# Where the K transposes of the next head stand in VectorE's program order

## The chip, the core and the metric

The kernel runs on one core of one Trainium2 chip. The metric is the device time in microseconds (us). Before the change, the first three runs took 420.04, 422.7 and 420.0 us (median 420.04).

## The reference, cut to what matters

Two layers work on a batch of four single tokens. Each layer is a grouped-query attention step over a long K and V cache, then a gated feed-forward block. Both layers read the same caches and weights.

```python
# B=4, Hq=32, Hkv=8, Sk=4096, Dh=128, D=512, F=1792, all bfloat16
def attention(x, k_cache, v_cache, wq, wo):
    q = heads(x @ wq)
    scores = einsum(q, repeat(k_cache)) * Dh ** -0.5
    o = einsum(softmax(scores), repeat(v_cache))
    return o @ wo
x = x + attention(layernorm(x), K, V, wq, wo)
x = x + glu(layernorm(x), w_gate, w_up, w_down)
x = x + attention(layernorm(x), K, V, wq, wo)
x = x + glu(layernorm(x), w_gate, w_up, w_down)
```

## The kernel before

One step of the main loop handles one KV head (called head n, 0 to 7 in layer 0 and 8 to 15 in layer 1). It needs four K tiles and four V tiles of 1 MiB, one for each batch row. The tiles live in a ring of 11 slots. A load is issued when a slot comes free, in the fixed order K(n), V(n), K(n+1), V(n+1), and so on. K slots come free after `scores(n)`, V slots after `values(n)`. Layer 1 walks the heads backwards, so that its first head (8) uses the tiles of head 7 again. These eight slots are therefore kept across the layers.

A small scheduler puts operations on engine queues in the order in which the Python code names them, and adds the semaphore waits that the data needs.

```python
ring = [sb(f"ring{i}", [P, T * DH], bf) for i in range(NS)]        # NS = 11

def done_with(n, kind):
    for b in range(B):
        if n == G - 1:                                   # head 7: kept for head 8
            slots[n + 1, kind, b] = slots[n, kind, b]
        else:
            free.append(slots[n, kind, b])
    pump()                                               # issues the next loads

def q_proj(n):
    ...                                                  # PE: Q_ps <- wq, xT
    S.put("act", ... qT[qi] <- Q_ps)
    ...                                                  # PE: Q_ps <- perm, qT
    S.put("act", ... qbd <- Q_ps)

def transpose_k(n, b):                                   # in place, as 32-bit words
    v = ring[slots[n, "k", b]][:].bitcast(dt.int32)
    S.put("dve", lambda e: e.transpose(v, v), ...)

def softmax(n):
    S.put("dve", ... ml <- max(S_ps))
    S.put("dve", ... nbias <- ml)
    S.put("act", ... p_sb <- exp(S_ps))

def weights(n):                                          # merges the four parts of a row
    S.put("dve", ... tr <- ml); S.put("dve", ... nM); S.put("dve", ... dd)
    S.put("act", ... ee <- exp(dd))
    S.put("dve", ... el, den, rden, wt, wcol)

# ... scores, probs_t, values, merge, merge_sum and y_proj are cut ...

def keys_of(n):
    if n != G:
        for b in range(B):
            transpose_k(n, b)
    scores(n); done_with(n, "k"); softmax(n); probs_t(n); weights(n)

def values_of(n):
    values(n); done_with(n, "v"); merge(n); merge_sum(n); y_proj(n)

for l in range(NLAYER):
    for n in range(l * G, (l + 1) * G - 2):
        keys_of(n)
        q_proj(n + 1)
        values_of(n)
    n = (l + 1) * G - 2
    keys_of(n); q_proj(n + 1); keys_of(n + 1); values_of(n); values_of(n + 1)
    # ... residual, feed-forward, next layer's norm and first q_proj ...
```

Of the kernel before, what the change touches and what calls it, by code (L numbers as in the profile page):

```python
# [91 lines left out]
def bass_interleave_layers__gqa_block_cached__glu_gated_glu__decode_kernel(nc, A_x, A_k, A_v, A_wq, A_wo, B_x, B_wg, B_wu, B_wd, out):  # L92
    B, SQ, D = A_x.shape
    _, G, SK, DH = A_k.shape
# [7 lines left out]
    NLAYER = 2  # L102
# [156 lines left out]
    def done_with(n, kind):  # L259


        for b in range(B):
            if n == G - 1:
# [3 lines that stand above are left out]
        pump()  # L267
# [102 lines left out]
    def layer_norm_q():  # L370
        layer_norm(mean_b, "mean_b", float(DH), rs_q, "rs_q")
# [4 lines left out]
    def q_proj(n):  # L376
        g = groups[n][1]
        qi = n % 2
        fns = []
        for h in range(R):  # L380
            for k in range(KD):
                c0 = (g * R + h) * DH
                fns.append(lambda e, h=h, k=k, c0=c0: e.matmul(  # L383
                    Q_ps[:, h * B:(h + 1) * B], lhsT=wq[:, k, c0:c0 + DH], rhs=xT[:, k, :],
                    start=(k == 0), stop=(k == KD - 1),
                ))
        S.put("pe", fns, reads=["xT", f"wq{g // 2}"], writes=["Q"])
        S.put("act", lambda e: e.activation(qT[qi][:], Q_ps[:, 0:R * B], ACTF.Copy), reads=["Q"], writes=[f"qT{qi}"])  # L388
        fns = []
        for n in range(NQ):  # L390
            fns.append(lambda e, n=n: e.matmul(  # L391
                Q_ps[:, 64 + n * 16:64 + (n + 1) * 16], lhsT=perm[:, n, :], rhs=qT[qi][:], start=True, stop=True,
            ))
        S.put("pe", fns, reads=[f"qT{qi}", "perm"], writes=["Q"])
        fns = []
        for a in range(4):
            fns.append(lambda e, a=a: e.activation(  # L397
                qbd[32 * a:32 * a + 32, qi, :, :, a * R:(a + 1) * R],
                Q_ps[32 * a:32 * a + 32, 64:128].rearrange("p (n h b) -> p b n h", n=NQ, h=R),
                ACTF.Copy,  # L400
            ))
        S.put("act", fns, reads=["Q"], writes=[f"qbd{qi}"])

    def transpose_k(n, b):
        s = slots[n, "k", b]
        v = ring[s][:].bitcast(dt.int32)
        S.put("dve", lambda e: e.transpose(v, v), reads=[f"r{s}"], writes=[f"r{s}"])  # L407

    def scores(n):
        qi = n % 2  # L410
        fns = []
        for q in range(2):
            for nn in range(NQ):
                for b in range(B):
                    kt = ring[slots[n, "k", b]][:].rearrange("p (t bb j r) -> p t bb j r", bb=2, j=32, r=2)
                    fns.append(lambda e, q=q, nn=nn, b=b, kt=kt: e.matmul(  # L416
                        S_ps[32 * b:32 * b + 16, q * 512:(q + 1) * 512],
                        lhsT=qbd[:, qi, b, nn, :],
                        rhs=kt[:, 16 * q:16 * q + 16, nn // 2, :, nn % 2],
                        start=(nn == 0), stop=(nn == NQ - 1),  # L420
                    ))
        S.put("pe", fns, reads=[f"qbd{qi}"] + [f"r{slots[n, 'k', b]}" for b in range(B)], writes=["S"])

    def softmax(n):
        S.put(
            "dve", lambda e: e.tensor_reduce(ml[:, 0:1], S_ps[:], AX.X, ALU.max, negate=True),  # L426
            reads=["S"], writes=["ml"],
        )
        S.put("dve", lambda e: e.tensor_scalar(nbias[:], ml[:, 0:1], rs_q[:], None, op0=ALU.mult),  # L429
              reads=["ml", "rs_q"], writes=["nbias"])  # L430
        S.put(
            "act",
            lambda e: e.activation(  # L433
                p_sb[:].rearrange("p tb (j q) -> p q tb j", q=4),
                S_ps[:].rearrange("p (q tb j) -> p q tb j", q=4, tb=8),
                ACTF.Exp, bias=nbias[:], scale=rs_q[:], accum_out=ml[:, 32:33],
            ),
            reads=["S", "nbias"], writes=["p_sb", "ml_l"],
        )

    def probs_t(n):
        pt = pt_sb[n % 2]
        fns = []
        for tb in range(8):
            fns.append(lambda e, tb=tb: e.matmul(  # L445
                PT_ps[:, tb * 64:(tb + 1) * 64], lhsT=p_sb[:, tb, :], rhs=sel_p[:], start=True, stop=True,
            ))
        S.put("pe", fns, reads=["p_sb", "sel_p"], writes=["PT"])
        S.put(
            "act", lambda e: e.activation(pt[:].rearrange("p t x -> p (t x)"), PT_ps[:], ACTF.Copy),  # L450
            reads=["PT"], writes=[f"pt_sb{n % 2}"],
        )

    def weights(n):
        S.put("dve", lambda e: e.transpose(tr[:], ml[:]), reads=["ml", "ml_l"], writes=["tr"])  # L455
        nm = tr[:, 0:16].rearrange("p (a h) -> p a h", h=R)
        ls = tr[:, 32:48].rearrange("p (a h) -> p a h", h=R)

        def bc(t):
            return t[:].unsqueeze(1).broadcast_to([P, 4, R])  # L460

        S.put(
            "dve",
            lambda e: e.tensor_reduce(nM[:], tr[:, 0:16].rearrange("p (a h) -> p h a", h=R), AX.X, ALU.min),
            reads=["tr"], writes=["nM"],
        )
        S.put("dve", lambda e: e.tensor_tensor(dd[:], bc(nM), nm, ALU.subtract), reads=["nM", "tr"], writes=["dd"])
        S.put("act", lambda e: e.activation(ee[:], dd[:], ACTF.Exp, scale=rs_q[:]), reads=["dd", "rs_q"],  # L468
              writes=["ee"])
        S.put("dve", lambda e: e.tensor_tensor(el[:], ee[:], ls, ALU.mult), reads=["ee", "tr"], writes=["el"])  # L470
        S.put(
            "dve", lambda e: e.tensor_reduce(den[:], el[:].rearrange("p a h -> p h a"), AX.X, ALU.add),
            reads=["el"], writes=["den"],
        )
        S.put("dve", lambda e: e.reciprocal(rden[:], den[:]), reads=["den"], writes=["rden"])
        S.put(
            "dve",
            lambda e: e.tensor_tensor(
                wt[:, 0:16].rearrange("p (a h) -> p a h", h=R), ee[:], bc(rden), ALU.mult
            ),  # L480
            reads=["ee", "rden"], writes=["wt"],
        )
        wc = wcol[n % 2]
        S.put("dve", lambda e: e.transpose(wc[:], wt[:]), reads=["wt"], writes=[f"wcol{n % 2}"])
# [27 lines left out]
    def merge_sum(n):  # L512

        _, g = groups[n]
        src = bass.AP(M_ps, 0, [[512, P], [32, B], [1, R], [P + R, 4]])
        dst = oT[:, g * R:(g + 1) * R, :].rearrange("p h b -> p b h")

        def fn(e):
            with nc.allow_low_precision("the heads' outputs enter the projection as bfloat16"):
                return e.tensor_reduce(dst, src, AX.X, ALU.add)  # L520

        S.put("dve", fn, reads=["M"], writes=[f"oT{g}"])

    def y_proj(n):
        _, g = groups[n]
        i = n % G
        fns = []
        for h in range(R):
            for j in range(4):
                fns.append(lambda e, h=h, j=j: e.matmul(  # L530
                    Y_ps[32 * j:32 * j + B, 0:P], lhsT=oT[:, g * R + h, :], rhs=wo[:, g * R + h, j * P:(j + 1) * P],
                    start=(i == 0 and h == 0), stop=(i == G - 1 and h == R - 1),
                ))
        S.put("pe", fns, reads=[f"oT{g}", f"wo{g // 2}"], writes=["Y"])
# [63 lines left out]
        residual(rs_h[:], ["rs_h"], last)  # L598


    def keys_of(n):

        if n != G:
            for b in range(B):
                transpose_k(n, b)
        scores(n)
        done_with(n, "k")
        softmax(n)
        probs_t(n)
        weights(n)  # L610

    def values_of(n):
        values(n)
        done_with(n, "v")
        merge(n)
        merge_sum(n)
        y_proj(n)

    layer_norm_q()
    q_proj(0)  # L620
    for l in range(NLAYER):
        for n in range(l * G, (l + 1) * G - 2):
            keys_of(n)
            q_proj(n + 1)
            values_of(n)
        n = (l + 1) * G - 2
        keys_of(n)
        q_proj(n + 1)
        keys_of(n + 1)
        values_of(n)  # L630
        values_of(n + 1)
        residual(1.0, [])
        glu(l == NLAYER - 1)
        if l < NLAYER - 1:
            layer_norm_q()
            q_proj(n + 2)
# [51 lines left out]
```

## Time and profile before

| | before |
|---|---|
| time, median of three | 420.04 us |
| layer 0, 10 to 210 us | 396 GB/s, DMA share 1.04 |
| layer 1, 240 to 340 us | 349 GB/s, DMA share 0.91 |
| start to start of the scores in layer 1 | 23.9 to 24.35 us |

These are three lines of the page of the kernel before: the busy line of the engines, then the DMA share (in tenths) and the GB/s in 40 slices of the span.

```profile
PE 165.4 (39%) x1998; PEld 69.7 (17%) x1998; DVE 192.5 (46%) x272; ACT 85.2 (20%) x171; POOL 9.4 (2%) x34
...
DMA  8999999999999999999940797979989797989220
GB/s 318 399 378 416 388 392 401 398 407 380 415 386 399 397 404 422 411 339 395 400 206 2 284 406 262 398 292 382 383 296 408 284 403 303 401 314 355 63 87 2
```

No engine is half busy. The loads run flat out in the first half. After a pause between the layers (slices 21 and 22) they swing between 262 and 408 GB/s, until they end.

The next lines are the stretches view of the kernel before. After the borders of a stretch and its length come the busy us (and instructions) of PE, PEld, DVE, ACT and POOL, the granted PE clock, the DMA share and GB/s.

```profile
10.00:210.00 200.00, 74.06 (x862) 30.24 (x866) 96.86 (x121) 39.78 (x81) 0.86 (x2) 0.63 1.04 396
240.00:340.00 100.00, 41.71 (x476) 16.89 (x472) 48.33 (x62) 20.80 (x41) 0.00 (x0) 0.58 0.91 349
```

Layer 0 is bound by loading, and layer 1 is not. In layer 0 it is a near tie: the scores of its heads 3 to 5 start 23.8 and 23.9 us apart (96.22, 120.06, 143.97), about the pace of layer 1, while the loads leave no gap. What holds layer 1 is read from the chain of waits of the kernel before, here for one head. The columns are start, length, and the work.

```profile
267.69 8.81 DVE ring L407 x4
...
276.54 3.62 PE S_ps L416 x31
...
280.18 1.24 DVE ml L426
...
281.74 2.63 ACT p_sb L433 x2
...
284.41 0.62 PE PT_ps L445 x8
...
286.25 3.56 PE O_ps L492 x31
...
289.91 0.70 ACT o_sb L504
...
290.65 1.13 PE M_ps L509 x4
...
291.81 0.23 DVE oT L520
292.03 2.21 DVE ring L407
```

This is a closed loop of compute with no load in it: transposes, scores, softmax, values, merge, and the next head's transposes. The four transposes are 8.8 of its 24.3 us. The waits view of the kernel before says the same. The columns are the total, the number of waits and the longest, in us.

```profile
PE S_ps L416 <- DVE ring L407: 132.5, 15, 11.2
...
PE Q_ps L391 <- ACT qT L388: 8.3, 16, 0.6
...
DVE ring L407 <- DMA ring<-in_A_k_cache_dram: 4.0, 9, 1.8
```

PE waits 132.5 us for transposes, and the transposes wait only 4.0 us for their data. This view is of the whole span: 73.1 of the 132.5 us lie between 10 and 210 us, in layer 0.

### The profile page before, as it was taken

Reading aid. Unit: us, or ns where it says so; the run is one execution under the profiler, and the core shown is the slowest. Engines: PE = TensorE matmul, PEld = TensorE weight load, DVE = VectorE, ACT = ScalarE, POOL = GpSimd, SP = SyncE. Lnnn points to the kernel's source line nnn. Section 1 sums busy time; section 2 is a strip of 40 time slices with the busy share of each in tenths; the row PEclk is TensorE's granted clock in tenths of the full one; section 3 lists DMA queues with packets and bytes.
Section 4 is the critical chain, followed back from the end, with each engine's and each line's share of the span. In section 5 each row is a group of like instructions: output and inputs, shape, how many; then the busy total and the mean of one; then the engine's idle time right before and its main releaser. Section 6 shows DMA issues by size and latency. Waiting matters only on the chain.

```text
span 418.9 us, 4800 instructions
## 1 busy us (share of the span) xinstructions
PE 165.4 (39%) x1998; PEld 69.7 (17%) x1998; DVE 192.5 (46%) x272; ACT 85.2 (20%) x171; POOL 9.4 (2%) x34
## 2 busy tenths in 40 slices
PE   0153350524435251405376514536251533531364
PEld 0121020201202020102134201103020210201022
DVE  3825418263452727392011272552728254466512
ACT  1040130402204040303011403103040302204031
POOL 6000000000000000000000000000000000000000
PEclk9985565666666566556565555565566666656579
DMA  8999999999999999999940797979989797989220
GB/s 318 399 378 416 388 392 401 398 407 380 415 386 399 397 404 422 411 339 395 400 206 2 284 406 262 398 292 382 383 296 408 284 403 303 401 314 355 63 87 2
DMA packets 48549, 140.04 MB, mean 334 GB/s; under 512 B 2192, under 2 KB 6544, under 8 KB 40848
## 3 DMA queue, kind: packets, MB, share of 16 engines
q1 hardware_dynamic: 48480, 139.73, 87.4%
q8 instruction: 16, 0.26, 0.3%
q14 instruction: 5, 0.04, 0.0%
q10 hardware_dynamic: 48, 0.01, 0.0%
HBM read 139.73 MB, written 0.00 MB: 334 GB/s over the span
## 4 chain that ended last, share of the span: by engine, by line
DVE 32%; PE 31%; DMA 14%; ACT 12%; SPq 6%; issue 3%; ACTq 0%; DVEq 0%
DVE ring L407 25%; PE S_ps L416 13%; DMA ring<-in_A_k_cache_dram 12%; PE O_ps L492 11%; ACT p_sb L433 9%; SPq L248 5%; DVE ml L426 4%; PE M_ps L509 2%; DMA ring<-in_A_v_cache_dram 2%; ACT o_sb L504 2%; PE PT_ps L445 2%; SPq L270 1%; ACT ee L468 1%; DVE nbias L429 1%; PE Q_ps L391 1%
## 5 line engine op out<-in xcount | busy, mean ns | idle before, releaser
L407 DVE STREAM_TRANSPOSE ring<-ring 128x2048 int32<-128x2048 int32 x60 | 134.1, 2282 | 4.0 <-DMA ring<-in_A_k_cache_dram 4.0
L416 PE MATMUL S_ps<-ring,qbd 128*16 128x512 bf16 x512 | 57.3, 623 | 133.5 <-DVE ring L407 132.5
L433 ACT ACTIVATE p_sb<-S_ps,nbias,rs_q 128x1024 bf16<-128x1024 f32 x16 | 41.8, 2613 | 232.4 <-DVE nbias L429 232.4
L492 PE MATMUL O_ps<-ring,pt_sb 128*16 128x512 bf16 x512 | 55.4, 609 | 5.7 <-DMA ring<-in_A_v_cache_dram 5.7
L426 DVE TENSOR_REDUCE ml<-S_ps 128x1 f32<-128x1024 f32 x16 | 19.6, 1224 | 61.0 <-PE S_ps L416 61.0
L416 PEld LDWEIGHTS S_ps<-ring,qbd 128*16 128x16 bf16 x512 | 15.7, 120 | 163.5 <-DVE ring L407 107.8
L520 DVE TENSOR_REDUCE oT<-M_ps 128x16 bf16<-128x64 f32 x16 | 3.6, 227 | 76.4 <-PE M_ps L509 76.4
L445 PE MATMUL PT_ps<-sel_p,p_sb 128*128 128x64 bf16 x128 | 9.7, 241 | 68.4 <-ACT p_sb L433 68.4
L455 DVE STREAM_TRANSPOSE tr<-ml 128x64 f32<-128x64 f32 x16 | 3.9, 245 | 43.7 <-ACT p_sb L433 43.7
L504 ACT ACTIVATE o_sb<-O_ps,wcol 128x512 f32<-128x512 f32 x16 | 11.0, 687 | 52.8 <-PE O_ps L492 52.8
L492 PEld LDWEIGHTS O_ps<-ring,pt_sb 128*16 128x16 bf16 x512 | 16.2, 121 | 32.0 <-issue 24.8
L445 PEld LDWEIGHTS PT_ps<-sel_p,p_sb 128*128 128x128 bf16 x128 | 7.2, 126 | 82.9 <-ACT p_sb L433 82.9
L509 PE MATMUL M_ps<-ident,o_sb 128*128 128x128 f32 x64 | 12.8, 333 | 13.8 <-ACT o_sb L504 13.8
L397 ACT ACTIVATE qbd<-Q_ps 32x64 bf16<-32x64 f32 x64 | 13.8, 215 | 6.4 <-PE Q_ps L391 5.9
L509 PEld LDWEIGHTS M_ps<-ident,o_sb 128*128 128x128 f32 x64 | 8.2, 164 | 27.7 <-ACT o_sb L504 27.7
L450 ACT ACTIVATE pt_sb<-PT_ps 128x512 bf16<-128x512 f32 x16 | 9.6, 597 | 11.2 <-PE PT_ps L445 11.2
L366 POOL TENSOR_TENSOR rs_h<-vpe,mhalf 128x1 f32<-128x1 f32 x2 | 1.1, 551 | 391.0 <-DVE vpe L362 205.3
L383 PE MATMUL Q_ps<-xT,wq 128*128 128x4 bf16 x256 | 9.4, 168 | 0.0
L530 PE MATMUL Y_ps<-wo,oT 128*4 128x128 bf16 x256 | 7.3, 244 | 5.1 <-DVE oT L520 5.1
L383 PEld LDWEIGHTS Q_ps<-xT,wq 128*128 128x128 bf16 x256 | 9.2, 109 | 0.0
L470 DVE TENSOR_TENSOR el<-ee,tr 128x16 f32<-128x16 f32 x16 | 2.8, 175 | 13.2 <-ACT ee L468 13.2
L391 PE MATMUL Q_ps<-qT,perm 128*128 128x16 bf16 x64 | 4.4, 179 | 8.3 <-ACT qT L388 8.3
(75 smaller groups left out, 84.7 us busy)
## 6 DMA issues: line engine op xcount, KB each, us to landing
ring<-in_A_k_cache_dram SPq DMA_DIRECT2D x60, 1024.0 KB, 12.7
ring<-in_A_v_cache_dram SPq DMA_DIRECT2D x60, 1024.0 KB, 14.0
wq<-in_A_wq_dram SPq DMA_DIRECT2D x4, 1024.0 KB, 14.2
wo<-in_A_wo_dram SPq DMA_DIRECT2D x4, 1024.0 KB, 14.6
wg<-in_B_w_gate_dram SPq DMA_DIRECT2D x1, 1792.0 KB, 16.3
wu<-in_B_w_up_dram SPq DMA_DIRECT2D x1, 1792.0 KB, 17.1
wd<-in_B_w_down_dram SPq DMA_DIRECT2D x1, 1536.0 KB, 23.3
wd_r<-in_B_w_down_dram SPq DMA_DIRECT2D x2, 128.0 KB, 21.1
```

Of the source, the lines that this page charges most:

```text
L248: S.put("sp", lambda e: e.dma_start(o, i), writes=[f"r{s}"], dma=f"r{s}")
L383: fns.append(lambda e, h=h, k=k, c0=c0: e.matmul(Q_ps[:, h * B:(h + 1) * B], lhsT=wq[:, k, c0:c0 + DH], rhs=xT[:, k, :], start=(k == 0), s ...
L397: fns.append(lambda e, a=a: e.activation(qbd[32 * a:32 * a + 32, qi, :, :, a * R:(a + 1) * R], Q_ps[32 * a:32 * a + 32, 64:128].rearrange( ...
L407: S.put("dve", lambda e: e.transpose(v, v), reads=[f"r{s}"], writes=[f"r{s}"])
L416: fns.append(lambda e, q=q, nn=nn, b=b, kt=kt: e.matmul(S_ps[32 * b:32 * b + 16, q * 512:(q + 1) * 512], lhsT=qbd[:, qi, b, nn, :], rhs=kt ...
L426: "dve", lambda e: e.tensor_reduce(ml[:, 0:1], S_ps[:], AX.X, ALU.max, negate=True),
L433: lambda e: e.activation(p_sb[:].rearrange("p tb (j q) -> p q tb j", q=4), S_ps[:].rearrange("p (q tb j) -> p q tb j", q=4, tb=8), ACTF.Ex ...
L445: fns.append(lambda e, tb=tb: e.matmul(PT_ps[:, tb * 64:(tb + 1) * 64], lhsT=p_sb[:, tb, :], rhs=sel_p[:], start=True, stop=True,))
L450: "act", lambda e: e.activation(pt[:].rearrange("p t x -> p (t x)"), PT_ps[:], ACTF.Copy),
L492: fns.append(lambda e, tb=tb, b=b, v=v: e.matmul(O_ps[32 * b:32 * b + 16, :], lhsT=pt[:, tb, 16 * b:16 * b + 16], rhs=v[:, :, tb, :], star ...
L504: "act", lambda e: e.activation(o_sb[:], O_ps[:], ACTF.Copy, scale=wc[:, 0:1]),
L509: fns.append(lambda e, a=a: e.transpose(M_ps[:, a * P:(a + 1) * P], o_sb[:, a * P:(a + 1) * P], ident[:]))
```

## The change

The intent is to do the next head's transposes in the time in which VectorE waits for other engines. One goes behind `nbias`, under the exponential on ScalarE. Two go behind `wcol`, under the values on PE. One stays behind `oT`. In the last pair of heads of a layer, all four are done inside the earlier head's `keys_of`. The first head's four are done up front. Instructions are neither added nor removed. Only VectorE's order changes; the orders of the other engines are the same.

```diff
-    def keys_of(n):
-        if n != G:
-            for b in range(B):
+    def tk(n, bs):
+        if n % G and n < NLAYER * G:
+            for b in bs:
                 transpose_k(n, b)
+
+    def keys_of(n, ahead):
         scores(n)
         done_with(n, "k")
         softmax(n)
+        tk(n + 1, ahead[:1])
         probs_t(n)
         weights(n)
-
-    def values_of(n):
+        tk(n + 1, ahead[1:])
+
+    def values_of(n, rest=()):
         values(n)
         done_with(n, "v")
         merge(n)
         merge_sum(n)
+        tk(n + 1, rest)
         y_proj(n)

     q_proj(0)
+    for b in range(B):
+        transpose_k(0, b)
     for l in range(NLAYER):
         for n in range(l * G, (l + 1) * G - 2):
-            keys_of(n)
+            keys_of(n, (0, 1, 2))
             q_proj(n + 1)
-            values_of(n)
+            values_of(n, (3,))
         n = (l + 1) * G - 2
-        keys_of(n)
+        keys_of(n, (0, 1, 2, 3))
         q_proj(n + 1)
-        keys_of(n + 1)
+        keys_of(n + 1, ())
         values_of(n)
         values_of(n + 1)
```

## The prediction

> **What bounds the kernel now.** The stretches view (10 us each) shows two regimes.
> Layer 0, 10 to 210 us: the DMA share is 1.00 to 1.08, at 397 GB/s on average. It is bound by loading: the Trainium skill ("DMA: Bandwidth & Descriptors", section "Where 436 GB/s comes from") puts the ceiling at 435 GB/s; the 421 of the best stretch agrees.
> Layer 1, 230 to 390 us: the DMA share falls to 0.71 to 0.89 in every second stretch (263 to 312 GB/s). The chain of waits there is compute alone, one head every 24.3 us, later 23.9: four K transposes 8.80, scores 3.62, maximum 1.24, nbias about 0.3, exponential 2.63, then about 1.8 to the start of values, values 3.6, o_sb 0.70, M 0.67 to 1.13, oT 0.23. A ring slot is freed only by scores or values, so this chain also holds back the loads: eight 1 MiB loads per head need about 20.8 us at the rates of full stretches (K 422 GB/s, V 385): a gap of about 3.5 us per head.
>
> **What the change does.** No instruction is added or removed: 60 transposes of 2.28 us stay on VectorE. Of the four for the next head, one goes behind nbias (hidden under the 2.63 us exponential), two behind wcol (4.5 us, where VectorE now waits about 4.7 us for M), and one stays behind oT, ahead of the scores. So about 6.6 us per head leave the compute chain, whose period becomes about 17.4 us. That is below the 20.8 us of loading, so layer 1 becomes bound by loading: the gain per head is 3.1 to 3.5 us, not 6.6. VectorE runs in order, so a transpose that waits for its K also holds up this head's weights. In the loading-bound stage that delays oT and the scores by about 1.5 us (estimate from these durations), but the loads have some 8 us of freed slots in hand: no gap from it.
>
> **Sum.** Layer 0 ends with the last V at 208.6 us, unchanged, and so does the transition to the end of layer 1's first scores at 231.5 us; the DMA gap there stays, since the last head's slots are kept for layer 1. From 231.9 us, 53 loads remain: 25 K at 2.48 us (spacing of K transposes that wait for their load) and 28 V at about 2.73: 138.5 us plus about 1.7 of start. The last V lands near 372, against its values starting at 405.9 now. Then values 3.6 us and a tail of 11 to 13 us (11.2 now; in layer 0 the same steps ran slower at a lower clock). Span about 388, time about 389 us: 7.4% faster.
>
> Predicted: 389 us, 8 in 10 within 383 to 398. Faster by over 2%: 0.95; within 2%: 0.04; slower: 0.01.
>
> **What would show it.** VectorE busy stays 192 to 193 us. Layer 0's last V still lands at 208 to 209 us. In layer 1 the DMA share is about 1.0 from 233 to 370 us, near 400 GB/s; the head period is 20.5 to 21.3 us. PE's waits for ring transposes (132.5 us, waits view) fall by a third to a half. The chain of waits turns from transposes to K and V loads in layer 1.
>
> **What would make it wrong.** If the delayed weights starve the ring (slots freed late), layer 0 passes 209 us and layer 1 keeps gaps: 395 to 405 us. If V loads at 410 GB/s when uninterrupted, 383 us.

## The result, and the profile after

The changed kernel took 393.72 us (median of four, 392.88 to 394.27), against 420.5 us of the kernel before (four runs, 420.0 to 422.7). The ratio is 0.9352, 95% interval 0.9313 to 0.939. Ratios here are the mean time of one kernel's fast runs over that of the other's of the same rounds, so not quite the ratio of the medians quoted. The profiled run took 393.91 us and has a span of 392.0 us.

The same lines of the page, of the changed kernel:

```profile
PE 168.5 (43%) x1998; PEld 71.5 (18%) x1998; DVE 191.6 (49%) x272; ACT 86.3 (22%) x171; POOL 9.4 (2%) x34
...
DMA  7999999999999999999999029999999999999900
GB/s 307 403 385 407 393 380 417 387 413 397 384 412 385 410 390 405 421 414 343 395 388 366 2 97 381 418 390 416 394 411 397 407 403 400 423 407 387 352 2 2
```

VectorE has as much work as before. The swings in the second half are gone. The stretches view of the changed kernel gives the two layers:

```profile
10.00:210.00 200.00, 77.09 (x862) 31.82 (x866) 95.78 (x121) 40.46 (x81) 0.86 (x2) 0.61 1.04 397
240.00:340.00 100.00, 46.73 (x560) 18.99 (x556) 59.38 (x75) 25.58 (x50) 0.00 (x0) 0.65 1.03 405
```

Layer 0 is as it was: the values of its last head start at 208.45 us, against 208.61 before. Layer 1 now loads at 405 GB/s instead of 349, with the share at 1.03. Its scores start at 262.44, 282.95, 303.85, 324.57 and 345.21 us in the timeline, so 20.5 to 20.9 us apart. The first two steps of layer 1 took only 17.7 and 17.3 us, which is the pace of the new compute chain.

The waits view of the changed kernel:

```profile
DVE ring L407 <- DMA ring<-in_A_k_cache_dram: 68.0, 11, 11.1
...
PE Q_ps L391 <- ACT qT L388: 66.5, 16, 10.7
...
ACT ee L468 <- DVE dd L467: 57.1, 10, 10.0
...
PE S_ps L416 <- DVE ring L407: 43.6, 15, 8.2
```

The first and the last line are the result: PE waits 43.6 us for transposes instead of 132.5, and the transposes now wait 68.0 us for their data. The two in the middle are something that the prediction did not have. They show again in the chain of waits of the changed kernel, for one head:

```profile
278.93 0.37 SPq L248
...
279.35 13.22 DMA ring<-in_A_k_cache_dram
...
292.59 2.31 DVE ring L407
...
295.06 0.19 DVE nM L464
...
295.54 0.31 ACT ee L468
...
295.97 0.28 PE Q_ps L391 x4
296.25 3.56 PE O_ps L492 x24
...
299.83 0.37 SPq L248
```

The loop now goes through a load. It also goes from VectorE (the weights) over ScalarE (`ee`) and PE's query projection to the values of the same head, although the values read nothing that the weights write. The timeline of the changed kernel shows how (start, length, engine, work; in brackets the idle time before it and what ended it):

```profile
130.22 0.60 ACT L450 ACTIVATE pt_sb<-PT_ps 128x512 bf16<-128x512 f32 x1 [0.70 <-PE PT_ps L445]
136.68 0.31 ACT L468 ACTIVATE ee<-dd,rs_q 128x16 f32<-128x16 f32 x1 [5.86 <-DVE dd L467]
136.89 0.16 ACT L388 ACTIVATE qT<-Q_ps 128x16 bf16<-128x16 f32 x1
...
137.11 0.27 PE L391 MATMUL Q_ps<-qT,perm 128*128 128x16 bf16 x4 [6.52 <-ACT qT L388]
137.33 3.59 PE L492 MATMUL O_ps<-ring,pt_sb 128*16 128x512 bf16 x32
```

The probabilities for the values are ready at 130.8 us (130.22 + 0.60), but the values start at 137.33. On PE they stand behind the next head's query projection. That waits for `qT` on ScalarE, which stands behind `ee`, which waits for `dd` on VectorE, which now stands behind a transpose that waits for its K. The Trainium skill ("PSUM — Partial Sum Buffer", section "Engine vs sequencer instructions") says that the queues of ScalarE and VectorE are strict FIFO and that PE's matmuls start in program order. This trace agrees: `qT` starts directly behind `ee`, after ScalarE has been idle for 5.86 us.

So two questions were left for experiments. Is the gain really the shorter of two periods giving way to the longer, in layer 1 alone? And does this unforeseen link cost anything?

### The profile page after: what moved, and what is told of

Read it like the earlier page. It is cut to its first block, busy times and chain, and to the rows that moved or that the text cites. A ratio compares the mean times of both kernels' runs of the same rounds, so it can differ in the third digit from the quotient of the medians.

```text
span 392.0 us, 4800 instructions
## 1 busy us (share of the span) xinstructions
PE 168.5 (43%) x1998; PEld 71.5 (18%) x1998; DVE 191.6 (49%) x272; ACT 86.3 (22%) x171; POOL 9.4 (2%) x34
## 4 chain that ended last, share of the span: by engine, by line
DMA 39%; PE 25%; DVE 18%; SPq 8%; ACT 7%; issue 2%; ACTq 0%; DVEq 0%
DMA ring<-in_A_k_cache_dram 36%; PE O_ps L492 13%; DVE ring L407 12%; PE S_ps L416 6%; SPq L248 5%; ACT p_sb L433 4%; SPq L270 3%; DMA ring<-in_A_v_cache_dram 2%; DVE ml L426 2%; ACT ee L468 1%; PE M_ps L509 1%; PE PT_ps L445 1%; ACT o_sb L504 1%; PE Y_ps L593 1%; PE Q_ps L391 1%
## 5 line engine op out<-in xcount | busy, mean ns | idle before, releaser
L407 DVE STREAM_TRANSPOSE ring<-ring 128x2048 int32<-128x2048 int32 x60 | 135.7, 2285 | 68.0 <-DMA ring<-in_A_k_cache_dram 68.0
L416 PE MATMUL S_ps<-ring,qbd 128*16 128x512 bf16 x512 | 56.6, 617 | 44.6 <-DVE ring L407 43.6
L391 PE MATMUL Q_ps<-qT,perm 128*128 128x16 bf16 x64 | 4.4, 179 | 66.5 <-ACT qT L388 66.5
L509 PE MATMUL M_ps<-ident,o_sb 128*128 128x128 f32 x64 | 13.7, 351 | 13.8 <-ACT o_sb L504 13.8
L468 ACT ACTIVATE ee<-dd,rs_q 128x16 f32<-128x16 f32 x16 | 4.9, 304 | 57.1 <-DVE dd L467 57.1
L391 PEld LDWEIGHTS Q_ps<-qT,perm 128*128 128x128 bf16 x64 | 3.0, 107 | 67.8 <-ACT qT L388 67.8
L450 ACT ACTIVATE pt_sb<-PT_ps 128x512 bf16<-128x512 f32 x16 | 9.6, 597 | 11.2 <-PE PT_ps L445 11.2
## 6 DMA issues: line engine op xcount, KB each, us to landing
wu<-in_B_w_up_dram SPq DMA_DIRECT2D x1, 1792.0 KB, 17.1
```

The lines of the kernel that those rows point to most:

```text
L407: S.put("dve", lambda e: e.transpose(v, v), reads=[f"r{s}"], writes=[f"r{s}"])
L416: fns.append(lambda e, q=q, nn=nn, b=b, kt=kt: e.matmul(S_ps[32 * b:32 * b + 16, q * 512:(q + 1) * 512], lhsT=qbd[:, qi, b, nn, :], rhs=kt ...
L509: fns.append(lambda e, a=a: e.transpose(M_ps[:, a * P:(a + 1) * P], o_sb[:, a * P:(a + 1) * P], ident[:]))
```

## The experiments

Two of the twelve kernels (6 and 7) compute a wrong attention. The record has all twelve as correct, these two as well, so the comparison with the reference is blunt for that part of the result. Kernels of experiments 1 to 4 ran on one chip, 5 to 8 on a second, 9 to 12 on a third, each beside runs of the kernel before.

### 1. The new order in layer 1 alone

```diff
-        tk(n + 1, ahead[:1])
+        lead = ahead[:1] if n // G == 1 else ()
+        tk(n + 1, lead)
...
-        tk(n + 1, ahead[1:])
+        tk(n + 1, ahead[len(lead):])
...
-            keys_of(n, (0, 1, 2))
+            c = 3 if l == 1 else 0
+            keys_of(n, tuple(range(c)))
...
-            values_of(n, (3,))
+            values_of(n, tuple(range(c, B)))
```

Expected: 

> The new order in layer 1 alone; in layer 0 the four transposes stand where they stood before (behind oT, and behind weights for the last head). Theory (layer 0 is bound by loading, so the change has nothing to win there): 393 to 395 us, the same as the changed kernel's 393.7 within 1 us. Rival (each layer gives half of the 26.8 us): 407 us.

Measured: 393.29 us (392.38 to 396.33), ratio 0.9383 (0.9331 to 0.9435). The whole gain is there with layer 1 alone.

### 2. The new order in layer 0 alone

The edit is the same with the layers exchanged.

Expected: 

> The new order in layer 0 alone; layer 1 in the order of before. Theory: 419 to 421 us, the same as before. Rival (each layer gives half): 407 us.

Measured: 419.84 us (418.07 to 422.29), ratio 0.9996 (0.9945 to 1.0046). Layer 0 gives nothing. The two runs together settle where the gain lies.

### 3. One transpose ahead instead of three

```diff
-            keys_of(n, (0, 1, 2))
+            keys_of(n, (0,))
             q_proj(n + 1)
-            values_of(n, (3,))
+            values_of(n, (1, 2, 3))
```

Expected: 

> Only one transpose ahead (behind nbias), three behind oT, in the regular steps. Theory (the longer of two periods counts: compute 24.1 - 2.28 = 21.9 us against 20.8 us of loading): layer 1's six steps from the first scores of head 8 to those of head 14 take about 131 us (144.6 before, 117.8 after), so 407 us, 1.5 either way. Rival (each transpose moved ahead is worth the same, a third of 26.8 us): 411.6 us.

Measured: 409.75 us (406.05 to 410.48), ratio 0.9734 (0.9682 to 0.9785). The median lies between the two theories' numbers, so the time alone does not decide. The trace does: the scores of head 8 start at 228.37 us and those of head 14 at 359.22, so six steps took 130.9 us, where the theory said about 131. In these steps no transpose waited for its load. The DMA share alone would not have shown that: from 240 to 340 us it is 1.02, and only the rate, 386 GB/s instead of 405, tells of it. The rest of the miss is not in these steps: head 8 started 1.0 us later than in the changed kernel (227.40), and from the scores of head 14 to the end it took 48.4 us (407.6 − 359.22) instead of 46.8 (392.0 − 345.21).

### 4. Two transposes ahead

```diff
-            keys_of(n, (0, 1, 2))
+            keys_of(n, (0, 1))
             q_proj(n + 1)
-            values_of(n, (3,))
+            values_of(n, (2, 3))
```

Expected: 

> Two transposes ahead (one behind nbias, one behind wcol), two behind oT. Theory: compute 24.1 - 4.55 = 19.6 us, already below 20.8 us of loading, so the third transpose moved buys nothing: 393 to 395.5 us, as the changed kernel. Rival (each one worth the same): 402.6 us.

Measured: 395.7 us (394.39 to 398.11), ratio 0.9424 (0.9376 to 0.9471). This is 0.2 us above the range of the theory and 7 us below the rival's number. The DMA share from 240 to 340 us is 1.03 at 404 GB/s, as in the changed kernel. Two transposes ahead are enough to make layer 1 bound by loading. Whether the third is worth 1 or 2 us is not resolved: the interval overlaps that of the changed kernel.

### 5. All four transposes ahead of the weights

```diff
-        tk(n + 1, ahead[:1])
+        tk(n + 1, ahead)
         probs_t(n)
         weights(n)
-        tk(n + 1, ahead[1:])
...
-            keys_of(n, (0, 1, 2))
+            keys_of(n, (0, 1, 2, 3))
             q_proj(n + 1)
-            values_of(n, (3,))
+            values_of(n)
```

Expected: 

> All four transposes of the next head stand behind nbias, so this head's weights, o_sb, M and oT wait for the whole next K to land. Theory (the ring's freed slots have some 8 us in hand, a late oT starves no load): loading still sets the pace, 393 to 397 us, DMA share about 1.0 in layer 1 from 240 us on. Rival (weights held back by transposes that wait for their K free slots late and make gaps in the loads): over 400 us, layer 0's last V later than 210 us.

Measured: 427.91 us (426.91 to 429.97), ratio 1.0191 (1.0139 to 1.0244), which is slower than the kernel before (whether by more than 2% is unclear). The theory failed here, by more than 30 us. Its stretches and waits views:

```profile
10.00:210.00 200.00, 57.10 (x790) 26.11 (x791) 96.11 (x113) 39.07 (x78) 0.86 (x2) 0.70 0.97 369
240.00:340.00 100.00, 38.88 (x502) 17.15 (x501) 51.60 (x64) 24.02 (x47) 0.55 (x1) 0.60 0.85 328
```

```profile
PE Q_ps L391 <- ACT qT L388: 151.3, 16, 16.6
ACT ee L468 <- DVE dd L467: 141.5, 14, 16.0
```

The loads have gaps in both layers (369 and 328 GB/s), and the values of layer 0's last head start at 223.13 us instead of 208.45. That is what the rival said. But the waits name the link of the section above, not the late `oT`: PE waits 151.3 us for `qT`. The values, and with them the release of four slots, wait for the whole next K to land. So there were two candidates for the starved ring, and experiment 9 was made to tell them apart.

### 6 and 7. Half of every V load, under both orders

Half of each V tile is loaded (0.5 MiB) and used twice, so that the engines do the same work with less loading. The same edit was made to the kernel before (6) and to the changed kernel (7).

```diff
+            i = i[:, 0:2]
-            o = dst[:].rearrange("p (a x) -> p a x", a=4)
+            o = dst[:].rearrange("p (a x) -> p a x", a=4)[:, 0:2]
...
-                    rhs=v[:, :, tb, :],
+                    rhs=v[:, 0:2, tb, :].unsqueeze(1).broadcast_to([P, 2, 2, DH]),
```

Expected of 6: 

> Wrong result on purpose: of every V tile only half is loaded (0.5 MiB) and used twice, the work of all engines is the same. Order of before. Theory (compute chain of 24.1 us binds): layer 1 as before, layer 0 about 10 us shorter: 409 us, 4 either way. If loading bound the kernel before in both layers, it would fall by about 25 us per 10 MB, to 380 us or less.

Expected of 7: 

> Wrong result on purpose: the same half V loads under the changed order. Theory (loading, 20.8 us per head, hides about half of the 6.6 us that left the compute chain): with loading at about 15.5 us per head the compute chain's period of 17.4 us appears in layer 1; time about 340 us, 330 to 350, so the order gains about 69 us against the half-V kernel in the order of before. Rival (the change itself is worth 27 us whatever the loads do): 382 us.

Measured: 409.76 us (408.28 to 411.13) in the order of before, and 341.78 us (340.54 to 343.84) in the new order. With less to load, the new order is worth 68 us instead of 27. The stretches from 240 to 340 us, first of 6, then of 7:

```profile
240.00:340.00 100.00, 41.93 (x480) 16.53 (x480) 48.46 (x61) 20.11 (x40) 0.00 (x0) 0.62 0.65 252
```

```profile
240.00:340.00 100.00, 52.55 (x650) 22.17 (x638) 55.27 (x81) 25.36 (x48) 0.55 (x1) 0.66 0.65 255
```

In neither are the loads the limit (share 0.65). The old order gained 11.5 us in layer 0 from the lighter loads (its last values start at 197.14 us instead of 208.61), which shows again how close the two periods were there. In 7 the scores of heads 11 to 14 start 17.1 to 17.3 us apart (241.96, 259.29, 276.47, 293.58), close to the 17.4 us that the prediction gave the new compute chain. In 6 they start 23.9 to 24.3 us apart. So about 6.7 us per head really left the compute chain, and in the real kernel loading hides about half of it.

### 8. The last two heads in another order

In the profile of the changed kernel the loads end near 372 us, but the values of the last head start at 376.41. This run moves the work of the last two heads of each layer.

```diff
# lines of the edit are joined by ; here
-        keys_of(n, (0, 1, 2, 3))
-        q_proj(n + 1)
-        keys_of(n + 1, ())
-        values_of(n)
+        scores(n); done_with(n, "k"); softmax(n)
+        tk(n + 1, (0, 1, 2, 3))
+        probs_t(n); q_proj(n + 1); weights(n)
+        scores(n + 1); done_with(n + 1, "k"); softmax(n + 1)
+        values(n); done_with(n, "v")
+        probs_t(n + 1); weights(n + 1)
+        merge(n); merge_sum(n); y_proj(n)
         values_of(n + 1)
```

Expected: 

> The changed kernel with the last two heads of each layer in another order: the four transposes of the last head stand behind nbias ahead of the weights, and values of head 14 run on PE under the softmax of head 15. Theory (the last V lands near 372 us, its values start only at 376.5 us for the order of the last two heads' work, which is where the prediction went short): values of head 15 start at 372 to 373 us, time 389 to 392 us, about 0.7% under the changed kernel. Rival (the tail is bound elsewhere): 393 to 395 us.

Measured: 392.79 us (392.31 to 393.11), ratio 0.9347 (0.9308 to 0.9386): the expected range of the time was missed by 0.8 us, and the interval does not set it apart from the changed kernel. The last values did start earlier, at 373.18 us. But they took 3.59 us instead of 1.90. The stretches view of the changed kernel, then of this one, from the start of the last values on:

```profile
376.40:380.60 4.20, 2.96 (x60) 1.38 (x52) 0.23 (x1) 0.69 (x1) 0.00 (x0) 1.00 0.02 4
```

```profile
373.10:376.80 3.70, 3.59 (x32) 1.08 (x32) 0.00 (x0) 0.00 (x0) 0.00 (x0) 0.50 0.02 4
```

The granted clock was 1.00 there in the changed kernel, where PE had been busy for 3.28 of the 4.4 us before, and 0.50 here, where PE had been idle for 2.5 us before. More than half of the earlier start was paid back in the values themselves. The Trainium skill ("TensorE: Matmul & The Clock Gate", section "Part 1: The HAM clock gate") says that the clock is granted by how busy PE has been just before; these two stretches agree with that, though no run here varied the idle time alone.

### 9. All four ahead of the weights, but without the link

This is experiment 5 with one more edit: the next head's query projection is issued before the weights. On ScalarE, `qT` then stands ahead of `ee`. PE's order does not change.

```diff
         probs_t(n)
+        if (n + 1) % G:
+            q_proj(n + 1)
         weights(n)
...
             keys_of(n, (0, 1, 2, 3))
-            q_proj(n + 1)
```

Expected: 

> The slow kernel with all four transposes ahead of the weights (427.9 us), with one thing moved: the query projection of the next head is issued ahead of the weights, so that on ScalarE the copy qT no longer stands behind the exponential ee of the weights. Theory A (what starved the ring was a hidden link: values on PE stand behind the query projection, which waits for qT, which stood behind ee, which waits for the transposes): values start about 2 us after the exponential ends, the gaps in the loads go, 393 to 398 us. Theory B (the late oT and scores alone starve the ring, as the rival of the earlier run said): 415 us or more.

Measured: 392.98 us, the median of the five fast runs (392.18 to 393.9), ratio 0.9347 (0.9315 to 0.9379). The sixth, the profiled one, took 619.38 us and is left out. Moving two small ScalarE operations (`qT` and `qbd`) took the kernel from 427.91 to 392.98 us. So the link was what starved the ring, and the late weights, `oT` and scores alone do not. What is missing is a trace of a fast run of this kernel: that its values start early is inferred from its order and from the trace of experiment 10.

### 10. The changed kernel without the link

The same edit was made to the changed kernel.

Expected: 

> The changed kernel with the query projection of the next head issued ahead of the weights: takes the same hidden link away there. Theory A (in the changed kernel the link makes values wait up to 11 us for the next head's first K, but inside the ring's slack, since the loads run without a gap): values start about 2 us after the exponential ends, time the same as the changed kernel, 392 to 395 us. Rival (the late values cost time in the changed kernel too): under 389 us.

Measured: 395.95 us (392.64 to 397.71), ratio 0.9407 (0.9362 to 0.9451). The median is 1 us above the expected range, and the interval overlaps that of the control below. Its timeline and its waits view show the link gone:

```profile
129.63 0.60 ACT L450 ACTIVATE pt_sb<-PT_ps 128x512 bf16<-128x512 f32 x1 [0.70 <-PE PT_ps L445]
130.12 0.18 ACT L388 ACTIVATE qT<-Q_ps 128x16 bf16<-128x16 f32 x1
...
136.73 0.31 ACT L468 ACTIVATE ee<-dd,rs_q 128x16 f32<-128x16 f32 x1 [5.16 <-DVE dd L467]
```

```profile
PE Q_ps L391 <- ACT qT L388: 5.6, 16, 0.4
```

The values of this head start at 130.57 us instead of 137.33, and PE's wait for `qT` is 5.6 us instead of 66.5. The loads run at 405 GB/s from 240 to 340 us, as with the link. In the changed kernel the link costs nothing that these runs can see.

### 11. The changed kernel again, as a control

Expected: 

> The changed kernel as it is, as a control on the same chip and in the same rounds: 392.5 to 394.5 us.

Measured: 394.41 us (391.17 to 396.83), ratio 0.938 (0.9335 to 0.9425), as expected. Experiments 9, 10 and 12 are compared with this one.

### 12. Both edits together

This is the changed kernel with the edits of 8 and 10.

Expected: 

> The changed kernel with both edits: query projection ahead of the weights, and the last two heads of each layer in the order of the tail run. Theory (loading ends near 372 us in all of them, and in the tail run an earlier start of the last values was paid back by a lower granted clock): 391 to 393.5 us, no more than 0.5% under the control. Rival (the two edits help each other): under 390 us.

Measured: 393.11 us (391.95 to 393.46), ratio 0.9345 (0.9313 to 0.9376), inside the expected range. It overlaps the control's interval. It beats the kernel before, but no experiment gave a version that beats the changed kernel clearly.

## Why the prediction was right or wrong

**What bounds each layer: right.** Layer 0 is bound by loading, though by little, and layer 1 was bound by the compute chain. Experiments 1 and 2 show that the whole gain is in layer 1.

**The two periods: right.** The prediction gave 17.4 us of compute and 20.8 us of loading per head. With less loading, 17.1 to 17.3 us showed (experiment 7). With full loading the heads are 20.5 to 20.9 us apart, after two steps of 17.7 and 17.3 us that the prediction did not have. Experiments 3, 4 and 7 show that the longer of the two sets the pace. The share of 1.0, near 400 GB/s, also came (1.03, 405 GB/s).

**The sum: 4.7 us too low, within the range.** The end of the loads was right (372 predicted; in the stretches view the DMA share is 1.05 to 1.06 up to 370 us, 0.95 in the next us, then 0.46 and 0.12). The prediction let the last values start then, at 372 us; they started at 376.41, because the compute chain of the last two heads, not a load, comes last there. They took 1.90 us instead of 3.6. The tail after them was 13.7 us (392.0 − 378.3) instead of 12, the middle of the 11 to 13 of the sum, and instead of 11.2 in the kernel before. The trace shows where: the first two blocks of matmuls of the feed-forward took 1.67 and 1.71 us, against 0.93 each before, at a granted clock of 0.57 (380.6 to 390 us) against 1.00 (407.65 to 415.9 us before). This differs between executions: in the profiled one of experiment 11, the same kernel, they took 0.93 us each and the tail 11.3. For the run shown the sum is 4.4 − 1.7 + 1.7 = 4.4 us of span; that the two sizes of 1.7 us cancel is chance. The mis-sized term that both executions show is the gap ahead of the last values (376.41 and 377.21 us), not the loading. A smaller part lies between the span and the time: 1.9 us (393.91 − 392.0) instead of about 1.

**The delayed weights: wrong in its path, right in its outcome.** The step that said a transpose waiting for its K "delays oT and the scores by about 1.5 us" was incomplete. It followed the data and not the queues. It missed that the values wait too, over `dd`, `ee`, `qT` and the query projection: 6.5 us in the head shown, up to 10.7 us. The statement "no gap from it" still held, because the ring had slack (experiment 10). As the step did not count this wait, that was in part luck: in experiment 5 a longer wait over the same path made gaps. How much slack was left can be estimated from the chain of waits after the change: from the issue of the next head's first K, 0.4 us after the end of the values, to its landing it takes 13.2 us, of which about 5.2 are the two loads that the freed slots start (2.73 + 2.48, as in the prediction) and about 1.7 the start of a load (the prediction's own estimate); the other 6 us are loads already released, which keep the DMA busy meanwhile. In experiment 5 the values wait for the whole next K, by this estimate the reserve is gone, and the kernel is slower than before.

**PE's waits for transposes: wrong in size.** They were to fall by a third to a half. They fell by two thirds, to 43.6 us. In its place PE now waits 66.5 us for `qT`, over the link that the prediction did not have.

**VectorE's busy time: 191.6 us,** just under the 192 to 193 predicted.

## What to carry to other kernels

When work is moved off a chain of compute, compare the chain's new period with the period of the loads per step. The gain stops at the longer one, and from there on a further move bought nothing that these runs resolve (experiment 4 against the changed kernel). When an instruction that waits for a load is put early in an in-order queue, follow the waits through every queue behind it, also where no data flows: here VectorE's wait reached the values over ScalarE's order, and a version with a longer wait (up to 16.6 us instead of 10.7) lost 34 us, which two ScalarE operations issued earlier brought back.

## What the Trainium skill lacked or had wrong

- "DMA: Bandwidth & Descriptors", section "Where 436 GB/s comes from", says that the HBM side (about 358 GB/s) binds for loads from HBM to SBUF. Here a core held 405 GB/s for 100 us, and 423 in the best slice of the page. The same page's remark that about 358 is each core's share when both cores of a pair stream fits better; that case was not run here. The prediction took the section's other figure, 435 GB/s for the SBUF ports, as the ceiling; no slice of a page here exceeds it.
- "Perfetto Trace Analysis", section "Identifying Dependency Chains", sends the reader to the semaphores that an instruction waits on. It does not say that a wait can be inherited through the program order of an engine in between. Here such a link made 66.5 us of PE waits, and 151.3 us in the worst kernel.
- "VectorE: DVE Perf Modes", section "The three transpose paths", gives a measured time for a 128x128 bf16 tile only. The 128x2048 transpose of 32-bit words took 2.27 to 2.31 us here, in every kernel.
- "TensorE: Matmul & The Clock Gate", section "Seeing it yourself", warns that records of the granted clock can be unreliable and that a quarter of full speed has been seen for over 50 us. In one execution out of six of the kernel of experiment 9, PE was slow from start to end: 619.38 us, with a block of scores taking 10.57 us at a recorded clock of 1.00, against 3.59 us in other kernels' fast runs, mostly at a recorded 0.50. The values took 10.63 us there at a recorded 1.00, and 1.90 us at the end of the changed kernel, also at a recorded 1.00, so the warning about the records fits. The slowdown, about 5.6 times, is more than the quarter that the page names, and the page has no case that lasts a whole kernel. The cause stays open.
